# A decode block on one core: two more engines run the attention loop, queries pass through two fixed tiles, and GpSimd's relays go

## The chip, the cores and the metric

The kernel runs on one core of one Trainium2 chip. The metric is device time of one execution in microseconds (us), lower is better. The engines are TensorE (PE in the profile; PEld is its weight load), VectorE (DVE), ScalarE (ACT), GpSimd (POOL) and SyncE (SP, which issues nearly all DMA loads). A trailing q, as in "DVEq", is an engine's sequencer.

## The reference, cut to what matters

```python
# B=2 sequences, one new token each; D=512; 32 query and 32 KV heads of 128; 8192 cached keys
q = layernorm(x) @ wq
scores = einsum("bhqd,bhkd->bhqk", q, k_cache) * 128**-0.5
o = einsum("bhqk,bhkd->bhqd", softmax(scores), v_cache)
h = x + o.reshape(B, 1, 4096) @ wo
y = layernorm(h)                                  # then a gated feed-forward block
g = y @ W_gate
return h + ((g * (g > 0)) * (y @ W_up)) @ W_down    # F = 1376
```

K and V are 134 MB each in bf16 and are read once. The arithmetic per byte is small.

## The kernel before

The 64 (sequence, head) problems are done as 32 "pairs" of two heads. Each pair has a K load and a V load of 4.2 MB each, into four slots (K into slots 0 and 2, V into 1 and 3). Of the 128 key columns per partition, VectorE computes 96 (a mult by the broadcast query, four halving adds, a reduce), and TensorE computes 32 (transposes, which ScalarE copies out of PSUM, then score matmuls). ScalarE takes the exponentials and TensorE multiplies by V ("PV"). Pairs 0 to 29 are a loop of 15 rounds on TensorE alone, while the other engines are unrolled. Pairs 30 and 31 are a separate tail, followed by the output projection and the feed-forward block.

```python
# TensorE, loop (before): GpSimd's semaphores g2p (query copied) and v2p (a K or V load has landed)
with nc.Fori(0, NI, engines=OrderedEngineSet([nc.tensor.engine])):
    k_part(body, 0, (1, 2, 3, 4), ((g2p, 1), (v2p, 1)))
    collect(body, 6)
    pv(body, 0, ((jd, J, ((v2p, 2), (a2p, 5))), (0, jd, ((a2p, 7),))))
    ...
# TensorE, tail: straight on the load's own semaphore
collect(tail, 1)
k_part(tail, P0, (2, 3, 4, 5), ((slot_sem[0], 256), (g2p, 1)))
...                                      # output projection of the first 30 heads
k_part(tail, P1, (9, 10, 11, 12, 14, 15, 16, 17), ((slot_sem[2], 256), (g2p, 2)))

# VectorE, unrolled, pair p
if p == P0:                              # pair 30: first the output of the last loop round
    o_norm(g - 1, t_ob_loop)             # waits for TensorE's collect
    o_spread(g - 1, dve)
dve.wait((slot_sem[s], 16 * (g + 1)), t_q_b)
dve.last()
...                                      # qv: the pair's query, broadcast
t_dm[p] = dve.run(nc.vector.tensor_tensor(out=prod[:, 0:jd, :], in0=k_t[:, 0:jd, :], in1=qv, op=ALU.mult))
...                                      # adds, reduce
# GpSimd, pair p: relays
for k in range(2):
    nc.gpsimd.wait_ge(slot_sem[s + k], 16 * (g + 1))
    nc.gpsimd.sem_inc(v2p, 1)
# SyncE, pair p: the slot is loaded again when the mult and TensorE's transposes have read it
sp.wait(t_dm[p], tokp("pt", p, NG - 1))
load(s, A_k_cache, p + 2)
```

The softmax here doesn't subtract the row's maximum and nothing guards it: scores larger than these inputs give would overflow.

Of the kernel before, what the change touches and what calls it, by code (L numbers as in the profile page):

```python
# [7 lines left out]
F32 = mybir.dt.float32  # L8
# [31 lines left out]
def bass_sequential_preLN__gqa_block_cached__glu_gated_reglu__decode_kernel(  # L40
# [34 lines left out]
    with ExitStack() as es:  # L75
# [15 lines left out]
        a2p, l2p, g2p, v2p = S("a2p"), S("l2p"), S("g2p"), S("v2p")  # L91
# [12 lines left out]
        q_b = sb("q_b", [128, NP * Dh], BF16)  # L104
        qT = sb("qT", [128, NP * 2], BF16)
        q2 = sb("q2", [128, NP, 2, 4], BF16)
        q2c = [sb(f"q2c{i}", [128, 2, 4], BF16) for i in range(2)]
# [12 lines left out]
        NS = 3  # L120
        scores = [sb(f"scores{i}", [128, JC], F32) for i in range(NS)]
# [40 lines left out]
        if True:  # L162

            def program():
# [91 lines left out]
                dve.run(nc.vector.memset(q2[:], 0.0))  # L256
                dve.wait(t)
                dve.last()
                for r in range(2):
                    for h in range(2):  # L260
                        t_q2 = dve.run(nc.vector.tensor_copy(
                            out=q2[64 * h:64 * h + 64, :, r, 2 * h:2 * h + 2],
                            in_=Sp[r][64 * h:64 * h + 64, 0:2 * NP].rearrange("p (n a) -> p n a", a=2)))
# [16 lines left out]
                for m in range(NP // 4):  # L280
                    if m >= 2:
                        dve.wait(t_mm[m - 2])
                    dve.last()
                    t = dve.run(nc.vector.tensor_copy(
                        out=qrep[m % 2].rearrange("p (k r) -> p k r", r=64),
                        in_=qT[:, m * 8:(m + 1) * 8].unsqueeze(2).broadcast_to([128, 8, 64])))
                    if m == 0:
                        t_mm = {}
                    pe.wait(t)
                    if m >= 2:  # L290
                        pe.wait(t_cp[m - 2])
                    for k in range(4):
                        i = nc.tensor.matmul(  # L293
                            Op[m % 2][:, k * 128:(k + 1) * 128], lhsT=qrep[m % 2][:, k * 128:(k + 1) * 128],
                            rhs=ident[:], start=True, stop=True)
                    t_mm[m] = pe.run(i)
                    act.wait(t_mm[m])
                    t_cp[m] = act.run(nc.scalar.activation(  # L298
                        out=q_b[:, m * 512:(m + 1) * 512], in_=Op[m % 2][:], func=ACT.Copy))
# [7 lines left out]
                                        skip_group_check=True))  # L307

# [17 lines left out]
                def k_part(T, p, ev, k_wait):  # L326
                    s, ng = (2 * p) % 4, split(p)[0]
                    k_t = tile(s)
                    wait = nc.tensor.wait_ge

                    def score(g):
                        wait(a2p, ev[g])
                        kv_ = kT[g % 2][:].rearrange("p (k n r) -> p k r n", n=128, r=2)
                        for k in range(GT // 2):
                            jj = g * GT + 2 * k
                            for r in range(2):
                                i = nc.tensor.matmul(  # L337
                                    Sp[p % 2][:, 2 * jj:2 * jj + 4], lhsT=kv_[:, k, r, :],
                                    rhs=q2c[p % 2][:, r, :], start=(r == 0), stop=(r == 1))
                        T.mark(("sc", p, g), i)  # L340
# [3 lines left out]
                    for g in range(ng):  # L344
# [7 lines left out]
                        T.mark(("pt", p, g), i)  # L352
# [4 lines left out]
                def pv(T, p, parts, between=None):  # L357
# [4 lines left out]
                    for j0, j1, waits in parts:  # L362
# [5 lines left out]
                        for j in range(j0, j1, VJ):  # L368
# [4 lines left out]
                                start=(q == 0 and n < 4), stop=(q == PG - 1 and n >= J // VJ - 4))  # L373
                            n += 1
                    T.mark(("pv", p), i)

                def collect(T, a):
# [5 lines left out]
                    T.mark("ob", i)  # L383

                def z_sum(T, bank):
                    T.mark("z", nc.tensor.matmul(  # L386
                        bank[:, ZC:ZC + 8], lhsT=ones_f[:], rhs=zs[:], start=True, stop=True))
# [9 lines left out]
                with nc.Fori(0, NI, engines=OrderedEngineSet([nc.tensor.engine])):  # L397
                    jd = split(0)[1]
                    k_part(body, 0, (1, 2, 3, 4), ((g2p, 1), (v2p, 1)))
                    collect(body, 6)  # L400
                    pv(body, 0, ((jd, J, ((v2p, 2), (a2p, 5))), (0, jd, ((a2p, 7),))))
                    k_part(body, 1, (8, 9, 10, 11), ((g2p, 2), (v2p, 3)))
# [3 lines left out]
                    pv(body, 1, ((jd, J, ((v2p, 4), (a2p, 12))), (0, jd, ((a2p, EV),))))  # L406
                    z_sum(body, Ob)
                    nc.tensor.sem_inc(g2p, -2)
                    nc.tensor.sem_inc(v2p, -4)
# [9 lines left out]
                k_part(tail, P0, (2, 3, 4, 5), ((slot_sem[0], 256), (g2p, 1)))  # L419
# [10 lines left out]
                for c in range(DC):  # L430
# [3 lines left out]
                k_part(tail, P1, (9, 10, 11, 12, 14, 15, 16, 17), ((slot_sem[2], 256), (g2p, 2)))  # L434
                pv(tail, P0, ((j30, J, ((slot_sem[1], 256), (a2p, 6))), (0, j30, ((a2p, 13),))))
                pv(tail, P1, ((j31, J, ((sem_vl[0], 16), (a2p, 18))), (0, j31, ((a2p, 19), (sem_vl[1], 16)))),
                   lambda: z_sum(tail, Sp[0]))
# [7 lines left out]
                def tokp(kind, p, *g):  # L445
                    return tok((kind, p) + g, p // 2)
# [17 lines left out]
                def normalize(bank, t_z):  # L464
                    dve.wait(t_z)
                    dve.run(nc.vector.tensor_reduce(
                        out=zr[:], in_=bank[:, ZC:ZC + 8].rearrange("p (n k) -> p n k", k=2), axis=AX.X, op=ALU.add))
                    dve.last()
                    dve.run(nc.vector.reciprocal(out=zi[:], in_=zr[:]))
                    dve.last()  # L470
# [7 lines left out]
                t_oc = {}  # L478

                def o_norm(g, t_ob):  # L480
                    normalize(Ob, t_ob)
                    t_oc[g] = dve.run(o_scale())

                def o_spread(g, prog):
                    e = prog.eng
                    prog.wait(t_oc[g], tok("og", g))
# [14 lines left out]
                def q_copy(p):  # L501
                    pool.wait(tokp("sc", p - 2, NG - 1) if p >= 2 else t_q2)
                    nc.gpsimd.tensor_copy(out=q2c[p % 2][:], in_=q2[:, p]).then_inc(g2p, 1)  # L503
# [5 lines left out]
                for p in range(NP):  # L509
                    s = (2 * p) % 4  # L510
                    k_t = tile(s)
# [3 lines left out]
                    if p == P0:  # L515
                        o_norm(g - 1, t_ob_loop)
                        o_spread(g - 1, dve)
                    dve.wait((slot_sem[s], 16 * (g + 1)), t_q_b)
                    dve.last()
                    qv = q_b[:, p * Dh:(p + 1) * Dh].unsqueeze(1).broadcast_to([128, jd, Dh])  # L520
                    t_dm[p] = dve.run(nc.vector.tensor_tensor(  # L521
                        out=prod[:, 0:jd, :], in0=k_t[:, 0:jd, :], in1=qv, op=ALU.mult))
                    w = Dh
                    while w > 8:
                        half = w // 2
                        dve.last()
                        dve.run(nc.vector.tensor_tensor(  # L527
                            out=prod[:, 0:jd, 0:half], in0=prod[:, 0:jd, 0:half], in1=prod[:, 0:jd, half:w], op=ALU.add))
                        w = half
                    dve.last()  # L530
                    sc = scores[p % NS]
                    t_s[p] = dve.run(nc.vector.tensor_reduce(out=sc[:, 0:jd], in_=prod[:, 0:jd, 0:w], axis=AX.X, op=ALU.add))  # L532
                    if p % 2 == 0 and 2 <= p < P0:
                        o_norm(g - 1, tok("ob", g))

                    if p < P0:
                        for k in range(2):
                            nc.gpsimd.wait_ge(slot_sem[s + k], 16 * (g + 1))
                            nc.gpsimd.sem_inc(v2p, 1)  # L539
                    if p % 2 == 0 and 2 <= p < P0:  # L540
                        o_spread(g - 1, pool)
                    if p < P1:
                        q_copy(p + 1)

                    def evacs(g0=0, g1=ng):
                        for gg in range(g0, g1):
# [3 lines left out]
                            elif p >= 1:  # L550
                                act.wait(tokp("sc", p - 1, NG - 2 + gg))
                            to_pe(nc.scalar.activation(  # L552
                                out=kT[gg % 2][:], in_=Tp[gg % 2][:].bitcast(BF16), func=ACT.Copy))

                    def exp_pe():
                        act.wait(tokp("sc", p, ng - 1), t_const)
                        exp(p, 0, lambda h, a: Sp[p % 2][h, 0:2 * ng * GT].rearrange(
                            "p (g j a) -> p g j a", a=2, j=VJ)[:, :, :, a])

                    def exp_dve(p, jd):  # L560
                        act.wait(t_s[p])
                        exp(p, 1, lambda h, a: scores[p % NS][h, 0:jd].rearrange("p (g j) -> p g j", j=VJ))

                    def sums():
                        if p >= 1:
                            act.wait(tokp("pv", p - 1))
                        to_pe(nc.scalar.activation(out=os_sb[:], in_=Op[0][:], func=ACT.Copy))  # L567

                    if p < P0:
                        evacs()  # L570
                        exp_pe()
                        if p % 2 == 0:
                            sums()
                        exp_dve(p, jd)
                    elif p == P0:
                        sums()
                        evacs()
                        exp_pe()
# [6 lines left out]
                    else:  # L585
                        evacs(0, NG)
                        exp_dve(P0, j30)
                        evacs(NG)
                        exp_pe()
                        exp_dve(P1, j31)  # L590

                    if p + 2 < NP:
                        sp.wait(t_dm[p], tokp("pt", p, NG - 1))
# [26 lines left out]
                normalize(Sp[0], tok("z", NI))  # L620
                to_pe(nc.scalar.activation(out=os_sb[:], in_=Op[0][:], func=ACT.Copy))
# [142 lines left out]
```

## Time and profile before

| | before |
|---|---|
| time, median of the first 3 runs | 662.32 us |
| DMA engines busy, per round of two pairs (38.85 us) | 1.00, at 431 to 432 GB/s |
| VectorE, TensorE, ScalarE busy per round | 28.7, about 19.5, 11.7 us |
| from a K load's issue to its landing | 32.3 us |

These are lines of the page of the kernel before. "busy us" gives each engine's busy time, its share and its instructions. The two rows of digits give, for 40 equal slices of the run, TensorE's granted clock in tenths and the busy share of the DMA engines. The last line is the chain of waits, by engine. The nines at the start of the clock row are not borne out by the work: from 84.2 to 123.1 us the view of stretches gives a clock of 1.00, but TensorE's 182 matmuls there take 20.38 us, as long as in a round at 0.50 (20.37 us).

```profile
span 660.9 us, 7674 instructions
...
PE 338.3 (51%) x3220; PEld 208.2 (31%) x3220; DVE 465.6 (70%) x282; ACT 198.9 (30%) x418; POOL 22.5 (3%) x121
...
PEclk9999999955556565655655565555565655555567
DMA  9999999999999999999999999999999999999996
...
DMA 80%; DVE 17%; PE 1%; SPq 1%; issue 0%; ACT 0%; DVEq 0%
```

Next is one round in the view of stretches of the kernel before. Its columns are the length, the busy time of each engine with instruction counts, the granted TensorE clock, the DMA share and GB/s.

```profile
core 0: us, PE busy (x) PEld busy (x) DVE busy (x) ACT busy (x) POOL busy (x), PEclk, DMA share, GB/s
...
278.50:317.30 38.80, 20.27 (x182) 12.36 (x174) 28.63 (x16) 11.68 (x25) 1.14 (x7) 0.50 1.00 432
```

The DMA is the only thing in this round with no idle time: a share of 1.00 at 432 GB/s, where VectorE, the busiest of the engines, works 28.63 of 38.80 us.

The timeline of the kernel before, around 290 us, shows how deep the queue is (start, duration, engine, line, operation, and in brackets the idle time before it and what ended that).

```profile
294.21 0.33 SPq L167 DMA_DIRECT2D slot<-in_A_k_cache_dram  x1
...
326.50 6.56 DVE L521 TENSOR_TENSOR prod<-slot,q_b 128x12288 bf16<-128x12288 bf16 x1 [4.63 <-DMA slot<-in_A_k_cache_dram]
...
326.66 1.06 PE L349 MATMUL T<-ident_f,slot 128*128 128x128 f32 x8 [1.69 <-POOLq L539]
```

The K load issued at 294.21 is used at 326.50, though 4.2 MB at 432 GB/s take only 9.7 us. Some 22 us of other loads lie ahead of it, and VectorE has waited 4.63 us for it. The waits of the kernel before, summed (us in total, times, longest), show the same: VectorE waits for K, and GpSimd, the relay, waits for V.

```profile
POOL q2c L503 <- DMA slot<-in_A_v_cache_dram: 221.3, 16, 19.4
...
DVE prod L521 <- DMA slot<-in_A_k_cache_dram: 150.7, 29, 14.2
...
PE T L349 <- POOLq L539: 51.4, 29, 10.3
```

This is the timeline of the tail before: collect (Ob), the transposes of pairs 30 and 31 (T), VectorE's normalization (zr) and mult of pair 30, the PV matmuls (O<-slot,e), and the down-projection (O<-slot,hd).

```profile
617.24 1.87 PE L380 MATMUL Ob<-sel,os_sb 128*128 128x4 f32 x8 [0.18 <-ACT os_sb L567]
...
618.97 1.95 PE L349 MATMUL T<-ident_f,slot 128*128 128x128 f32 x8
619.15 0.17 DVE L466 TENSOR_REDUCE zr<-Ob 128x4 f32<-128x8 f32 x1 [6.19 <-PE Ob L380]
...
620.26 6.55 DVE L521 TENSOR_TENSOR prod<-slot,q_b 128x12288 bf16<-128x12288 bf16 x1
...
632.10 1.69 PE L349 MATMUL T<-ident_f,slot 128*128 128x128 f32 x8
...
643.37 4.06 PE L370 MATMUL O<-slot,e 128*16 128x512 bf16 x48
...
647.68 1.04 PE L370 MATMUL O<-slot,e 128*16 128x512 bf16 x16
...
657.38 1.02 PE L717 MATMUL O<-slot,hd 128*2 128x128 bf16 x24 [0.51 <-DMA slot<-in_B_W_down_dram]
```

At the very end TensorE waits for the last weights: the DMA stream ends the run.

### The profile page before, as it was taken

How to read it: one execution, taken by the hardware profiler on the slowest of the kernel's cores; microseconds unless marked ns; L12 is line 12 of the kernel's file. 1: busy time of each engine (PE TensorE's matmuls, PEld its weight loads, DVE VectorE, ACT ScalarE, POOL GpSimd, SP SyncE). 2: the span in 40 equal slices, each digit the busy share in tenths (PEclk: the TensorE clock that was granted, in tenths of full speed). 3: DMA queues.
4: the chain of work that ended last, by engine and by line, in shares of the span. 5: the costliest groups of instructions: out<-in, count | busy, mean ns of one | idle time of the engine just before them, and what ended most of it. 6: DMA issues, size and time to landing. Idle time of an engine off the chain costs nothing.

```text
span 660.9 us, 7674 instructions
## 1 busy us (share of the span) xinstructions
PE 338.3 (51%) x3220; PEld 208.2 (31%) x3220; DVE 465.6 (70%) x282; ACT 198.9 (30%) x418; POOL 22.5 (3%) x121
## 2 busy tenths in 40 slices
PE   2653354546555354545535464554446454445787
PEld 2431332224333122333313233332324232232464
DVE  1766576788767678776768867676886767787691
ACT  0521321233332133333213333222323322232360
POOL 2000000000000000000000000000000000000000
PEclk9999999955556565655655565555565655555567
DMA  9999999999999999999999999999999999999996
GB/s 381 426 417 428 440 421 438 430 428 438 423 436 432 428 440 420 438 433 424 440 422 436 436 423 438 425 432 436 426 435 428 432 432 430 434 431 428 440 416 270
DMA packets 10787, 281.23 MB, mean 426 GB/s; under 512 B 1202, under 2 KB 1556, under 8 KB 1940
## 3 DMA queue, kind: packets, MB, share of 16 engines
q1 hardware_dynamic: 10760, 281.06, 99.1%
q8 instruction: 6, 0.10, 0.1%
q14 instruction: 9, 0.07, 0.0%
q10 hardware_dynamic: 12, 0.00, 0.0%
HBM read 281.05 MB, written 0.00 MB: 425 GB/s over the span
## 4 chain that ended last, share of the span: by engine, by line
DMA 80%; DVE 17%; PE 1%; SPq 1%; issue 0%; ACT 0%; DVEq 0%
DMA slot<-in_A_k_cache_dram 76%; DVE prod L521 16%; DMA slot<-in_B_W_down_dram 4%; DVE prod L527 1%; PE O L370 0%; PE Ob L380 0%; PE O L717 0%; DVE scores L532 0%; SPq L167 0%; SPq L609 0%; ACT e L457 0%; ACT os_sb L567 0%; SPq L173 0%; SPq L176 0%; SPq L613 0%
## 5 line engine op out<-in xcount | busy, mean ns | idle before, releaser
L521 DVE TENSOR_TENSOR prod<-slot,q_b 128x12288 bf16<-128x12288 bf16 (+1 forms) x32 | 207.7, 6492 | 152.4 <-DMA slot<-in_A_k_cache_dram 150.7
L527 DVE TENSOR_TENSOR prod<-prod 128x6144 bf16<-128x6144 bf16 (+4 forms) x128 | 210.2, 1642 | 4.4
L370 PE MATMUL O<-slot,e 128*16 128x512 bf16 x1024 | 118.2, 615 | 185.5 <-ACT e L457 129.7
L552 ACT ACTIVATE kT<-T 128x1024 bf16<-128x1024 bf16 x132 | 131.2, 1022 | 194.8 <-PE T L349 191.1
L349 PE MATMUL T<-ident_f,slot 128*128 128x128 f32 x528 | 126.7, 401 | 51.4 <-POOLq L539 51.4
L349 PEld LDWEIGHTS T<-ident_f,slot 128*128 128x128 f32 x528 | 91.6, 206 | 65.7 <-issue 65.7
L370 PEld LDWEIGHTS O<-slot,e 128*16 128x16 bf16 x1024 | 26.1, 112 | 251.8 <-ACT e L457 157.3
L457 ACT ACTIVATE e<-scores 64x96 bf16<-64x96 f32 (+1 forms) x64 | 19.4, 303 | 210.2 <-DVE scores L532 209.8
L337 PE MATMUL S<-q2c,kT 128*128 128x4 bf16 x1056 | 50.0, 169 | 37.6 <-ACT kT L552 37.5
L337 PEld LDWEIGHTS S<-q2c,kT 128*128 128x128 bf16 x1056 | 43.3, 107 | 66.5 <-ACT kT L552 64.6
L380 PE MATMUL Ob<-sel,os_sb 128*128 128x4 f32 x136 | 31.0, 351 | 24.9 <-ACT os_sb L567 24.2
L380 PEld LDWEIGHTS Ob<-sel,os_sb 128*128 128x128 f32 x136 | 29.5, 320 | 26.8 <-ACT os_sb L567 25.6
L532 DVE TENSOR_REDUCE scores<-prod 128x96 f32<-128x768 bf16 (+1 forms) x32 | 30.2, 945 | 1.1
L457 ACT ACTIVATE e<-S 64x32 bf16<-64x32 f32 (+1 forms) x64 | 13.0, 204 | 14.8 <-PE S L337 14.4
L503 POOL COPY q2c<-q 128x8 bf16<-128x8 bf16 x32 | 7.6, 238 | 235.3 <-DMA slot<-in_A_v_cache_dram 221.3
L457 ACT ACTIVATION_READ_ACCUMULATOR e<-S 64x1 f32 x64 | 12.8, 201 | 0.7
L489 POOL MEMSET O_l<- 128x40 bf16 (+1 forms) x13 | 1.8, 136 | 315.4 <-DVE O_cur L473 315.4
L457 ACT ACTIVATION_READ_ACCUMULATOR e<-scores 64x1 f32 x64 | 11.8, 184 | 0.0
L386 PEld LDWEIGHTS Ob<-zs,ones_f 128*128 128x128 f32 x30 | 7.2, 300 | 12.7 <-issue 12.7
L567 ACT ACTIVATE os_sb<-O 128x512 f32<-128x512 f32 x16 | 9.6, 597 | 3.2 <-PE O L370 2.8
L298 ACT ACTIVATE q_b<-O 128x512 bf16<-128x512 f32 x8 | 4.3, 594 | 17.9 <-PE O L293 17.9
L386 PE MATMUL Ob<-zs,ones_f 128*128 128x8 f32 x30 | 8.6, 361 | 0.0
(93 smaller groups left out, 83.6 us busy)
## 6 DMA issues: line engine op xcount, KB each, us to landing
slot<-in_A_k_cache_dram SPq DMA_DIRECT2D x32, 4096.0 KB, 32.3
slot<-in_A_v_cache_dram SPq DMA_DIRECT2D x31, 4096.0 KB, 30.6
slot<-in_A_wq_dram SPq DMA_DIRECT2D x1, 4096.0 KB, 12.4
slot<-in_A_v_cache_dram SPq DMA_DIRECT2D x2, 2048.0 KB, 28.0
X<-in_A_wo_dram SPq DMA_DIRECT2D x1, 3840.0 KB, 46.9
slot<-in_B_W_up_dram SPq DMA_DIRECT2D x1, 1376.0 KB, 23.7
slot<-in_B_W_gate_dram SPq DMA_DIRECT2D x1, 1376.0 KB, 26.7
slot<-in_B_W_down_dram SPq DMA_DIRECT2D x2, 512.0 KB, 28.8
```

Source lines behind the costliest of these rows:

```text
L337: i = nc.tensor.matmul(Sp[p % 2][:, 2 * jj:2 * jj + 4], lhsT=kv_[:, k, r, :], rhs=q2c[p % 2][:, r, :], start=(r == 0), stop=(r == 1))
L349: i = nc.tensor.transpose(Tp[g % 2][:, k * 128:(k + 1) * 128], k_t[:, j:j + 2, :].rearrange("p j d -> p (j d)").bitcast(F32), ident_f[:])
L370: i = nc.tensor.matmul(Op[0][c:c + 16, :], lhsT=e_t[q][:, j // VJ, :], rhs=v_t[:, j:j + VJ, :].rearrange("p j d -> p (j d)"), start=(q == ...
L380: i = nc.tensor.matmul(Ob[:, 0:4], lhsT=os_sb[:, jj * Dh:(jj + 1) * Dh], rhs=sel[:, 4 * jj:4 * jj + 4], start=(jj == 0), stop=(jj == VJ - 1))
L386: T.mark("z", nc.tensor.matmul(bank[:, ZC:ZC + 8], lhsT=ones_f[:], rhs=zs[:], start=True, stop=True))
L457: i = nc.scalar.activation(out=e_t[q][h, j0 // VJ:j1 // VJ, 8 * q:8 * q + 8].rearrange("p g (j a) -> p g j a", a=2)[:, :, :, a], in_=src(h ...
L503: nc.gpsimd.tensor_copy(out=q2c[p % 2][:], in_=q2[:, p]).then_inc(g2p, 1)
L521: t_dm[p] = dve.run(nc.vector.tensor_tensor(out=prod[:, 0:jd, :], in0=k_t[:, 0:jd, :], in1=qv, op=ALU.mult))
L527: dve.run(nc.vector.tensor_tensor(out=prod[:, 0:jd, 0:half], in0=prod[:, 0:jd, 0:half], in1=prod[:, 0:jd, half:w], op=ALU.add))
L532: t_s[p] = dve.run(nc.vector.tensor_reduce(out=sc[:, 0:jd], in_=prod[:, 0:jd, 0:w], axis=AX.X, op=ALU.add))
L552: to_pe(nc.scalar.activation(out=kT[gg % 2][:], in_=Tp[gg % 2][:].bitcast(BF16), func=ACT.Copy))
L567: to_pe(nc.scalar.activation(out=os_sb[:], in_=Op[0][:], func=ACT.Copy))
```

## The change

The intent is to put VectorE and ScalarE into the same 15-round loop, so that the program is short. The loop body is written with fixed addresses, the same in every round. The query of a pair (8 columns for TensorE, 128 for VectorE) is therefore copied by GpSimd into one of two fixed tiles, and waits count inside a round and are reset at its end. VectorE itself now tells TensorE that K has landed (k2p), and TensorE waits for V directly. GpSimd relays nothing any more. The core of the diff:

```diff
-        q_b = sb("q_b", [128, NP * Dh], BF16)
+        QW = 8 + Dh
+        q_all = sb("q_all", [128, NP, QW], BF16)
-        q2c = [sb(f"q2c{i}", [128, 2, 4], BF16) for i in range(2)]
+        q_c = [sb(f"q_c{i}", [128, QW], BF16) for i in range(2)]
 ...
-                    k_part(body, 0, (1, 2, 3, 4), ((g2p, 1), (v2p, 1)))
+                    k_part(body, 0, (1, 2, 3, 4), ((k2p, 1),))
 ...
-                k_part(tail, P0, (2, 3, 4, 5), ((slot_sem[0], 256), (g2p, 1)))
+                k_part(tail, P0, (2, 3, 4, 5), ((k2p, 1),))
-                k_part(tail, P1, (9, 10, 11, 12, 14, 15, 16, 17), ((slot_sem[2], 256), (g2p, 2)))
+                k_part(tail, P1, (9, 10, 11, 12, 14, 15, 16, 17), ((k2p, 2),))
 ...
+                with nc.Fori(0, NI, engines=OrderedEngineSet([nc.vector.engine])):
+                    for q in range(PG):
+                        nc.vector.wait_ge(g2d, q + 1)
+                        nc.vector.wait_ge(slot_sem[2 * q], 16)
+                        nc.vector.sem_inc(k2p, 1)
+                        last_d()
+                        run_d(k_mult(q))
+                        last_d()
+                        nc.vector.sem_inc(d2s, 1)
+                        k_adds(q, run_d, last_d)
+                        if q == 0:
+                            nc.vector.wait_ge(p2d, 1)
+                            normalize(Ob, run_d, last_d)
 ...
+                        run_d(k_reduce(q))
+                        last_d()
+                        nc.vector.sem_inc(d2a, 1)
+                    for sem, n in ((d2d, n_d[0]), (g2d, PG), (p2d, 1), (slot_sem[0], 16), (slot_sem[2], 16)):
+                        nc.vector.sem_inc(sem, -n)
 ... (ScalarE: the same kind of loop over evacuations and exponentials)
-                    if p < P0:
-                        for k in range(2):
-                            nc.gpsimd.wait_ge(slot_sem[s + k], 16 * (g + 1))
-                            nc.gpsimd.sem_inc(v2p, 1)
 ... (VectorE, tail, pairs 30 and 31)
+                    if p >= P0:
+                        if p == P0:
+                            dve.wait(t_ob_loop)
+                            normalize(Ob, dve.run, dve.last)
+                            o_spread(g - 1, dve, dve.run(o_scale()))
+                        nc.vector.wait_ge(g2d, p - P0 + 1)
+                        nc.vector.wait_ge(slot_sem[s], 16)
+                        nc.vector.sem_inc(k2p, 1)
 ...
-                        sp.wait(t_dm[p], tokp("pt", p, NG - 1))
+                        sp.wait((d2s, p + 1), tokp("kf", p))
```

## The prediction

> **What bounds the kernel now.** The DMA engines. The table of busy time by stretches of 19.4 us (one pair) shows a DMA share of 1.00 and 429 to 432 GB/s in all thirty stretches from 45 to 628 us. [...] The page's 281.23 MB at 432 GB/s are 651 us (an estimate) of the span of 660.9; the rest is the start (381 GB/s) and about 3 us after the last weights land.
>
> All compute idles in each period. VectorE is busy 14.2 us of 19.4 per pair (mult 6.56, adds 3.36, 1.76, 0.96, 0.56, reduce 0.95); in the waits it waits 150.7 us for K over 29 mults. TensorE is busy 9.8, ScalarE 5.8. The queue is deep: in the timeline a K load is issued right after the mult that frees its slot (294.21) and lands 32.3 us later, though moving its 4 MB takes 9.7. Some 22 us of other loads lie ahead of it: a slot freed up to 20 us later would not starve the DMA.
>
> **What the change does.**
> - VectorE and ScalarE run 15 rounds of a loop. Bytes and tensor work stay; the loop adds a branch, five semaphore resets on VectorE and two on ScalarE per round of 38.85 us. Estimate from the gaps of dependent instructions (0.02 to 0.05 us each): below 1 us a round, inside VectorE's 4.6 to 5.1 us idle per pair.
> - Normalization (0.15 + 0.18 + 0.16 us, about 0.55 with gaps) moves ahead of the reduce of even pairs; exp and the second part of PV come 0.6 us later there. PV now ends at 325.0, the next K lands at 326.5: still in time.
> - TensorE's transposes are released by VectorE reaching the pair, not by GpSimd. VectorE already waits when K lands.
> - The K slot is released at group 2's first score rather than after the last transposes: about 1 us later.
> - GpSimd copies 136 instead of 8 elements per pair (0.19 to 0.34 us now, perhaps 0.4), a pair ahead. Its waits for V (221 us) cost nothing.
> - The mult reads its query 16 bytes into a fixed tile. [...] I expect 6.56 us; no trace here shows it yet. [...]
>
> **On the critical path:** practically nothing. The chain names K loads 76% and the mult 16%, but that mult time passes while the queue is full.
>
> **Prediction:** 662.3 us, 8 in 10 between 661.2 and 664.0. Faster by over 2%: 0.01; within 2%: 0.97; slower by over 2%: 0.02.
>
> **What would show it.** Right: DMA share 1.00 at 432 GB/s in every pair, 38.85 us per round, mult 6.56 us, VectorE waiting for K 4 to 5 us per pair, TensorE's "POOLq" waits gone, last weights landing near 657. Wrong: a stretch with DMA share below 1, mult near 13 us, VectorE idle before a mult for GpSimd's copy or instruction fetch.
>
> **What would make it wrong.** Refetching a loop body behind a saturated DMA, costing over 5 us per pair; GpSimd's query copy, VectorE and TensorE taking turns instead of running a pair ahead; a later tail on VectorE, whose last exp (645.2) precedes V's last half (647.4) by only 2 us.

Two passages are cut from it, and the cuts marked, because no trace or run here shows what they state: a figure for the highest DMA rate, and an argument about the query's offset in its tile with what the mult would cost if it failed. Neither was a term of the forecast. The 662.3 us are the 662.32 us of the kernel before with nothing added, since all extra work was put into idle time. As to the risk of refetching: the pages do list instruction fetches among the DMA queues (15 packets, 0.17 MB before; 10 packets, 0.13 MB after), but that a loop body is fetched again in each round is shown by no trace.

## The result, and the profile after

| | before | after |
|---|---|---|
| time, median | 662.17 us (4 runs, 661.84 to 662.89) | 663.80 us (4 runs, 663.57 to 664.15) |
| ratio | | 1.0024, 95% interval 1.0006 to 1.0041 |

A ratio here is the mean time of one kernel's runs over that of the other's of the same rounds, so it is not quite the ratio of the medians. In the later sets the recorded ratios come out only if the profiled run of the edited kernel is left out (for e1_p0_early, below, its slowest: with it the means give 1.0017 instead of 1.0011). 663.80 lies inside the predicted 661.2 to 664.0, in its upper part. The 1.6 us are still worth a search.

The page of the changed kernel, the same lines as before:

```profile
span 662.3 us, 7890 instructions
...
PE 331.6 (50%) x3221; PEld 200.0 (30%) x3221; DVE 467.6 (71%) x285; ACT 215.9 (33%) x432; POOL 71.9 (11%) x121
...
PEclk9995565555756556755555567555675555557557
DMA  9999999999999999999999999999999999999995
...
DMA 76%; DVE 16%; PE 5%; ACT 2%; issue 1%; SPq 0%; DVEq 0%; ACTq 0%
```

One round of the changed kernel, in the view of stretches:

```profile
278.50:317.30 38.80, 20.35 (x178) 12.33 (x174) 28.73 (x16) 12.95 (x26) 4.53 (x7) 0.50 1.00 432
```

The round is the same: DMA share 1.00, 432 GB/s, VectorE 28.7 us. Two things are new and idle-filling. ScalarE is busy 1.3 us longer and GpSimd 3.4 us longer. Both are in the timeline of the changed kernel:

```profile
294.13 0.33 SPq L168 DMA_DIRECT2D slot<-in_A_k_cache_dram  x1
294.19 6.74 DVE L529 TENSOR_TENSOR prod<-prod 128x6144 bf16<-128x6144 bf16 x4
294.23 3.48 POOL L516 COPY q_c<-q_all 128x136 bf16<-128x136 bf16 x1 [10.90 <-DVEq L572]
...
302.78 1.28 ACT L547 ACT_TABLE_LOAD   x1
...
321.89 0.30 POOL L516 COPY q_c<-q_all 128x136 bf16<-128x136 bf16 x1
...
326.31 1.97 PE L358 MATMUL T<-ident_f,slot 128*128 128x128 f32 x8 [0.61 <-DVEq L568]
326.34 6.56 DVE L520 TENSOR_TENSOR prod<-slot,q_c 128x12288 bf16<-128x12288 bf16 x1 [4.28 <-DMA slot<-in_A_k_cache_dram]
```

The mult takes 6.56 us as before. VectorE still waits 4.28 us for K, and TensorE's transposes start at the same moment as the mult. The same query copy on GpSimd takes 0.30 us once and 3.48 us the other time, when it starts 0.04 us after VectorE's first add (3.36 us) and ends 0.16 us after it; in the whole run 15 copies take 3.48 us. The four adds are not slower for it (6.74 us, and 6.73 us before). ScalarE now loads its function table in every round (15 loads of 1.28 us in the loop, where the kernel before had one). Neither cost shows in the DMA column.

The waits of the changed kernel answer to those of before. GpSimd's waits for V are gone, VectorE's for K are nearly as long, and TensorE's transposes wait for VectorE's sequencer, in the loop and once in the tail (L620).

```profile
DVE prod L520 <- DMA slot<-in_A_k_cache_dram: 142.9, 29, 14.1
...
PE T L358 <- DVEq L568: 29.1, 28, 9.9
...
PE T L358 <- DVEq L620: 0.9, 1, 0.9
```

The last loop round is not late: the mult of pair 29 starts at 598.36 us (before: 598.62). So the extra time is in the tail. The timeline of the tail after:

```profile
617.13 1.87 PE L394 MATMUL Ob<-sel,os_sb 128*128 128x4 f32 x8 [0.17 <-ACT os_sb L550]
...
619.03 0.17 DVE L482 TENSOR_REDUCE zr<-Ob 128x4 f32<-128x8 f32 x1 [6.25 <-PE Ob L394]
...
619.95 1.97 PE L358 MATMUL T<-ident_f,slot 128*128 128x128 f32 x8 [0.95 <-DVEq L620]
...
620.14 6.55 DVE L520 TENSOR_TENSOR prod<-slot,q_c 128x12288 bf16<-128x12288 bf16 x1
...
633.62 1.97 PE L358 MATMUL T<-ident_f,slot 128*128 128x128 f32 x8
...
645.16 4.88 PE L382 MATMUL O<-slot,e 128*16 128x512 bf16 x48
...
650.29 1.04 PE L382 MATMUL O<-slot,e 128*16 128x512 bf16 x16
...
658.58 1.28 PE L791 MATMUL O<-slot,hd 128*2 128x128 bf16 x40
```

TensorE waits 0.95 us for VectorE to finish normalizing and spreading, and the down-projection no longer waits for a landing. The two tails, step by step (starts of the same instructions):

| step | before | after | difference |
|---|---|---|---|
| transposes of pair 30 start | 618.97 | 619.95 | +0.98 |
| from there to the transposes of pair 31 | 13.13 | 13.67 | +0.54 |
| from there to PV of pair 30 | 11.27 | 11.54 | +0.27 |
| from there to the last 16 PV matmuls | 4.31 | 5.13 | +0.82 |
| from there to the first down-projection matmul (656.17, 658.52) | 8.49 | 8.23 | -0.26 |
| from there to the end (device times of these two runs, 662.11 and 663.57) | 5.94 | 5.05 | -0.89 |

The sum is +1.46 us, the difference of the two profiled runs. The first line is the wait. The next four (+1.37) go mostly with TensorE's granted clock; about 0.13 us of the +0.54 is pair 31 held by VectorE (13.67 us, against 13.54 in f3_both below, without that gate at the same half speed). Between 628 and 633 us it was 0.84 before and 0.50 after; between 643 and 650 us, 0.78 and 0.54; between 650 and 657 us, 0.71 and 0.95. The last line is the wait for weights (0.51 us on TensorE's matmuls and 0.33 on its weight load), which is gone because TensorE now comes later. So, as an estimate from these lines, TensorE's chain could have been about 0.9 us later before the change at no cost.

### The profile page after: what moved, and what is told of

It reads as the page before. It is cut to its first block, busy times and chain, and to the rows that moved or that the text cites. A ratio compares the mean times of both kernels' runs of the same rounds, so it can differ in the third digit from the quotient of the medians. Undisturbed runs are those within 1.5% of the kernel's fastest.

```text
span 662.3 us, 7890 instructions
## 1 busy us (share of the span) xinstructions
PE 331.6 (50%) x3221; PEld 200.0 (30%) x3221; DVE 467.6 (71%) x285; ACT 215.9 (33%) x432; POOL 71.9 (11%) x121
## 4 chain that ended last, share of the span: by engine, by line
DMA 76%; DVE 16%; PE 5%; ACT 2%; issue 1%; SPq 0%; DVEq 0%; ACTq 0%
DMA slot<-in_A_k_cache_dram 76%; DVE prod L520 15%; PE O L382 1%; PE T L358 1%; DVE prod L529 1%; ACT kT L547 1%; PE O L442 1%; PE Ob L394 0%; PE S L341 0%; PE W L448 0%; ACT e L474 0%; PE O L739 0%; PE S L739 0%; PE O L791 0%; ACT os_sb L550 0%
## 5 line engine op out<-in xcount | busy, mean ns | idle before, releaser
L520 DVE TENSOR_TENSOR prod<-slot,q_c 128x12288 bf16<-128x12288 bf16 (+1 forms) x32 | 207.7, 6492 | 144.9 <-DMA slot<-in_A_k_cache_dram 142.9
L358 PE MATMUL T<-ident_f,slot 128*128 128x128 f32 x528 | 117.6, 379 | 30.2 <-DVEq L568 29.1
L358 PEld LDWEIGHTS T<-ident_f,slot 128*128 128x128 f32 x528 | 84.7, 194 | 45.6 <-DVEq L568 44.5
L516 POOL COPY q_c<-q_all 128x136 bf16<-128x136 bf16 x32 | 57.1, 1788 | 198.2 <-DVEq L572 168.0
L341 PE MATMUL S<-q_c,kT 128*128 128x4 bf16 x1056 | 49.2, 169 | 39.2 <-ACT kT L547 38.5
L341 PEld LDWEIGHTS S<-q_c,kT 128*128 128x128 bf16 x1056 | 41.1, 105 | 68.0 <-ACT kT L547 66.6
L299 ACT ACTIVATE q_all<-O 128x512 bf16<-128x512 f32 x8 | 4.4, 596 | 17.9 <-PE O L294 17.9
## 6 DMA issues: line engine op xcount, KB each, us to landing
slot<-in_A_k_cache_dram SPq DMA_DIRECT2D x32, 4096.0 KB, 32.1
```

Of the source, the lines that this page charges most:

```text
L341: i = nc.tensor.matmul(Sp[p % 2][:, 2 * jj:2 * jj + 4], lhsT=kv_[:, k, r, :], rhs=q_c[p % 2][:, 4 * r:4 * r + 4], start=(r == 0), stop=(r ...
L358: i = nc.tensor.transpose(Tp[g % 2][:, k * 128:(k + 1) * 128], k_t[:, j:j + 2, :].rearrange("p j d -> p (j d)").bitcast(F32), ident_f[:])
L516: nc.gpsimd.tensor_copy(out=q_c[p % 2][:], in_=q_all[:, p]).then_inc(g2d, 1)
L520: return nc.vector.tensor_tensor(out=prod[:, 0:jd_, :], in0=tile((2 * p) % 4)[:, 0:jd_, :], in1=q_c[p % 2][:, 8:QW].unsqueeze(1).broadcast ...
```

## The experiments

**Theory A:** TensorE's tail has two new gates. Pair 30 waits for VectorE's normalization and spread of the last round. Pair 31 waits until VectorE has got through pair 30 (its reduce starts at 633.50, TensorE's pair 31 at 633.62). They make TensorE's chain, and not the DMA, end last. **Theory L:** the loops cost it, a little per round (table loads, longer copies, branches). **Theory C:** it is only where TensorE's full-speed stretches fall in the tail.

### First set, one chip: the gates removed, and the gates alone

e1_p0_early, the edit in the changed kernel:

```diff
+                        nc.vector.wait_ge(g2d, p - P0 + 1)
+                        nc.vector.wait_ge(slot_sem[s], 16)
+                        nc.vector.sem_inc(k2p, 1)
                         if p == P0:
                             dve.wait(t_ob_loop)
                             normalize(Ob, dve.run, dve.last)
                             o_spread(g - 1, dve, dve.run(o_scale()))
-                        nc.vector.wait_ge(g2d, p - P0 + 1)
-                        nc.vector.wait_ge(slot_sem[s], 16)
-                        nc.vector.sem_inc(k2p, 1)
```

> The changed kernel, but in the tail VectorE releases TensorE for pair 30 before it normalizes and spreads the last loop round's output, not after. Theory A (the 1.5 us come from the tail: TensorE's chain there ends last, because both its pairs are now released by VectorE's program order): pair 30's transposes start near 619.0 us instead of 619.95, but pair 31's still wait until VectorE has dispatched pair 30's reduce (633.5), so the time stays within 0.4 us of the changed kernel (663.8). Theory L (the loops cost it, a little in each round): same time as the changed kernel, and the same for the next two kernels. Theory C (nothing but the phase of TensorE's granted clock in the tail): no change that is owed to the edit; the time follows the clock that the profile shows after 618 us.

e2_both_early does the same for pair 30, and in VectorE's adds of pair 30:

```diff
+                        if p == P0 and w == Dh // 4:      # second add issued
+                            nc.vector.wait_ge(g2d, 2)
+                            nc.vector.wait_ge(slot_sem[2], 16)
+                            nc.vector.sem_inc(k2p, 1)
```

> As e1_p0_early, and pair 31 is released after pair 30's second add was issued (about 630 us). Theory A: pair 31's transposes start near 632.6 instead of 633.6, the chain of TensorE ends about 1 us earlier: 662.2 to 663.0, near the kernel before (662.2). Theory L: 663.8 as the changed kernel. Theory C: 663.8, moved only by the clock.

e3_before_gated puts the two gates, and nothing else, into the kernel before:

```diff
-                k_part(tail, P0, (2, 3, 4, 5), ((slot_sem[0], 256), (g2p, 1)))
+                k_part(tail, P0, (2, 3, 4, 5), ((slot_sem[0], 256), (g2p, 1), (k2p, 1)))
 ... (pair 31 likewise, with (k2p, 2))
                     dve.wait((slot_sem[s], 16 * (g + 1)), t_q_b)
+                    if p >= P0:
+                        nc.vector.sem_inc(k2p, 1)
```

> The kernel before, no loops on VectorE and ScalarE, no fixed query tile, GpSimd's relays kept; TensorE only waits in the tail, in addition, until VectorE has reached pair 30 (after normalization and spread) and pair 31. Theory A: 0.7 to 1.6 us slower than the kernel before, near 663.5, and TensorE no longer waits for the down-projection weights. Theory L and theory C: same time as the kernel before (662.2) within 0.3 us, apart from the clock.

| run | this, median (range) | kernel before, same rounds | ratio, 95% interval |
|---|---|---|---|
| e1_p0_early | 663.11 (662.10 to 664.53) | 662.03 | 1.0011 (0.9998 to 1.0025) |
| e2_both_early | 661.29 (660.79 to 661.62) | 662.03 | 0.9985 (0.9971 to 0.9998) |
| e3_before_gated | 663.26 (661.91 to 663.48) | 662.03 | 1.0011 (0.9998 to 1.0025) |

Removing both gates took more than the whole 1.6 us away with the loops, table loads and copies still in place; at 661.29 it is even below the 662.2 to 663.0 that theory A had allowed. Adding the gates to the kernel before, which has none of those, made it about 1 us slower, though the interval just reaches 1. That speaks for A and against L. In the trace of e3_before_gated the wait appears where A puts it (timeline), and the wait for the down-projection weights is gone, as expected:

```profile
619.70 1.94 PE L350 MATMUL T<-ident_f,slot 128*128 128x128 f32 x8 [1.01 <-DVEq L521]
```

In e1_p0_early the transposes of pair 30 started at 619.02, as expected, and those of pair 31 were held by VectorE until 633.79 (timeline). What pair 30 gained, pair 31 gave back.

```profile
619.02 1.95 PE L358 MATMUL T<-ident_f,slot 128*128 128x128 f32 x8
...
633.79 1.97 PE L358 MATMUL T<-ident_f,slot 128*128 128x128 f32 x8 [1.09 <-DVEq L616]
```

The median, 0.7 us under the changed kernel's first result, missed the expected 0.4. But e1's times run over 2.4 us, so an effect of half a microsecond can't be read from five of them.

### Is the slack of the loop real? Extra work on VectorE

e4_pad3, in the loop of the changed kernel, puts half a mult in front of the mult; e5_pad7 instead issues run_d(k_mult(q)) and last_d() once more. The edit of e4_pad3:

```diff
+                        run_d(nc.vector.tensor_tensor(
+                            out=prod[:, :, 0:64], in0=tile(2 * q)[:, 0:JC, 0:64],
+                            in1=q_c[q][:, 8:72].unsqueeze(1).broadcast_to([128, JC, 64]), op=ALU.mult))
+                        last_d()
                         run_d(k_mult(q))
                         last_d()
```

> The changed kernel with an extra half mult on VectorE in each of the 30 loop pairs (about 3.36 us, result overwritten by the full mult). By the account that VectorE has 4.3 to 5 us idle per pair and K's slot some 20 us of queue slack: rounds stay 38.85 us apart with DMA share 1.00, and only the last round's 3.4 us show in the tail: 666 to 668 us. If time followed VectorE's work per round instead (no slack): 663.8 + 30 x 3.4 = 765 us.

> The changed kernel with the full mult issued twice in each of the 30 loop pairs: VectorE needs about 21.0 us per pair, over the 19.4 that the DMA needs. By the account: VectorE becomes the limit, never waits for K after the first rounds, DMA share falls to about 0.92, and the time to 700 to 715 us (26 + 30 x 21 + 50).

e4_pad3 took 667.00 us (665.67 to 667.49), a ratio of 1.0068 (1.0052 to 1.0083). That is 3.2 us over the changed kernel for 101 us of added VectorE work. The same stretch as above, in e4_pad3:

```profile
278.50:317.30 38.80, 17.26 (x178) 9.75 (x174) 35.44 (x18) 12.74 (x26) 4.54 (x7) 0.63 1.00 432
```

VectorE is busy 35.44 of 38.80 us and the DMA share is still 1.00. Only the last round's extra half mult, which nothing follows in the loop, reaches the end: TensorE's collect in the tail starts at 620.19, 3.06 us later than in the changed kernel. This bears out the prediction's account of the loop for VectorE, and it speaks against theory L: the extra work of 29 pairs vanishes. It does not test ScalarE's slack, where the table loads are. For those the evidence is the DMA share of 1.00 in every round, pair 29 starting no later than before, and e2_both_early, which keeps them all and is not slower than the kernel before.

e5_pad7 went over the slack, as meant, and missed its number: 743.49 us (one run, state unknown), not 700 to 715. VectorE became the limit and the DMA share fell to 91.9%. The VectorE timeline of e5_pad7, two starts of a round's first mult and the second pair's between them:

```profile
294.86 13.15 DVE L520 TENSOR_TENSOR prod<-slot,q_c 128x12288 bf16<-128x12288 bf16 x2 [1.24 <-DVEq L586]
...
316.89 13.15 DVE L520 TENSOR_TENSOR prod<-slot,q_c 128x12288 bf16<-128x12288 bf16 x2 [0.29 <-POOL q_c L516]
...
339.14 13.15 DVE L520 TENSOR_TENSOR prod<-slot,q_c 128x12288 bf16<-128x12288 bf16 x2 [1.23 <-DVEq L586]
```

A round takes 44.28 us, 22.14 a pair, where I had put 21.0. The missing 1.1 us a pair are the normalization (0.76 us a round), the idle time at the round's end (1.24 us), 0.29 us between its two pairs, which is a wait for GpSimd's query copy, and gaps. Thirty pairs times 1.1 us are 34 of the 37 us between the time and the sum 26 + 30 x 21 + 50. So the loop's end, with its five semaphore resets, does cost VectorE about 1.2 us per round here, and in the changed kernel that lies in idle time (VectorE waits 5.00 us for K before a round's first mult, at 306.91 us).

### Second and third set: is it the gates or the clock?

r1_after_again is the changed kernel unedited, and r2_e1_again is the kernel of e1_p0_early. Both ran on a second chip together with e6_late_small.

> The changed kernel, nothing edited, beside the next two on one chip, and a second profile of its tail. Theory A: again about 1.6 us over the kernel before, TensorE's transposes of pair 30 after VectorE's spread, the end set by TensorE and not by a landing. If the granted clock in the tail falls differently than in its first profile (half from 616 to 649.7), the time should move by up to 1 us with it.

> The kernel of e1_p0_early again, to tell its 663.1 from the changed kernel's 663.8 on one chip. Theory A: within 0.4 us of r1_after_again, since pair 31 still waits for VectorE's reduce of pair 30. If it is clearly faster (over 0.4 us), releasing pair 30 alone has a worth that the account misses.

e6_late_small is e2_both_early with two small loads moved from the start to behind the last V load. The reason is a line of the timeline of e2_both_early: TensorE, early now, waits 2.03 us for the last half of V.

```profile
641.54 2.77 PE L382 MATMUL O<-slot,e 128*16 128x512 bf16 x48
...
646.65 1.67 PE L382 MATMUL O<-slot,e 128*16 128x512 bf16 x16 [2.03 <-DMA slot<-in_A_v_cache_dram]
```

```diff
-                nc.sync.dma_start(wo_last[:]...).then_inc(sem_wl, 16)      # at the start
-                nc.sync.dma_start(wd_last[:], ...).then_inc(sem_wd[3], 16)
 ... (after both halves of V of pair 31)
+                        nc.sync.dma_start(wo_last[:]...).then_inc(sem_wl, 16)
+                        nc.sync.dma_start(wd_last[:], ...).then_inc(sem_wd[3], 16)
```

> As e2_both_early, and the loads of the last two heads' output weights and the last 96 rows of the down-projection (352 KB) are issued behind V of pair 31 instead of at the start. If the end of e2_both_early is set by the landing of V's last half (TensorE waited 2.0 us for it), that half lands 0.8 us earlier (estimate: 352 KB at 432 GB/s), and the time falls by 0.3 to 0.9 us, to about 660.6, unless the down-projection weights then land last. If TensorE or VectorE sets the end, no change.

A third chip then ran all four combinations of the two gates side by side. f2_p1_only is e2_both_early with pair 30's release back behind the spread.

> The changed kernel again, first corner of a table of four on one chip: pair 30 released late or early, pair 31 released late or early. Theory A: about 663.4, TensorE's output projection of the FFN (the start of the down-projection matmuls) some 5.0 us before the time, as in all profiles of kernels whose end TensorE sets.

> Second corner: only pair 30 released early. Theory A as first put says within 0.4 us of f0_none; the two earlier sets of five gave 0.7 less on average. If it is again 0.4 to 0.9 us less, the account has to be widened (pair 30's gate moves where the full-speed stretches of TensorE's clock fall, or gives time that pair 31's gate does not take back); if not, the earlier difference was the clock's chance.

> Third corner: pair 30 released late as in the changed kernel, only pair 31 early. Theory A: TensorE gets to pair 31 at about 633.6 by itself, so its early release is worth nothing alone: within 0.3 us of f0_none.

> Fourth corner: both early. Theory A: 661.3 again, about 2 us under f0_none, more than the two single edits together, because each gate hides behind the other.

| set | run | this, median (range) | before, median | ratio, 95% interval |
|---|---|---|---|---|
| second | r1_after_again | 663.00 (662.58 to 663.66) | 661.95 | 1.0019 (1.0005 to 1.0032) |
| second | r2_e1_again | 662.24 (662.18 to 663.07) | 661.95 | 1.0005 (0.9992 to 1.0019) |
| second | e6_late_small | 661.08 (660.65 to 661.15) | 661.95 | 0.9982 (0.9969 to 0.9996) |
| third | f0_none | 662.65 (660.51 to 663.60) | 662.14 | 0.9996 (0.9980 to 1.0012) |
| third | f1_p0_only | 663.07 (662.15 to 663.85) | 662.14 | 1.0012 (0.9999 to 1.0024) |
| third | f2_p1_only | 662.44 (661.29 to 663.86) | 662.14 | 1.0004 (0.9992 to 1.0016) |
| third | f3_both | 662.26 (661.27 to 662.97) | 662.14 | 0.9998 (0.9985 to 1.0011) |

The third set did not bear out the clear picture of the first. The same changed kernel ran twice in 660.5 to 660.6 us and four times in 662.6 to 663.6. The kernel with both gates removed was no faster there than with them, where about 2 us had been expected. So I had taken the first set for more than it was. In the second set r2_e1_again was 0.76 us under r1_after_again, outside the expected 0.4; in the third, f1_p0_only was 0.42 us above f0_none. No gain from pair 30 alone is left of that. f2_p1_only lay 0.2 us from f0_none, as expected. Pooled over the three chips (mean, standard error, range):

| kernel | runs | mean | range |
|---|---|---|---|
| before | 33 | 662.18 ± 0.07 | 661.62 to 663.14 |
| changed (first result, r1, f0) | 15 | 662.95 ± 0.28 | 660.51 to 664.15 |
| pair 30 early (e1, r2, f1) | 15 | 662.90 ± 0.20 | 662.10 to 664.53 |
| pair 31 early (f2) | 6 | 662.44 ± 0.38 | 661.29 to 663.86 |
| both early (e2, f3) | 10 | 661.76 ± 0.23 | 660.79 to 662.97 |
| before with the gates (e3) | 5 | 662.98 ± 0.29 | 661.91 to 663.48 |

The pooled order is the one theory A expects: pair 30 alone is worth nothing, both together about 1.2 us, with a standard error near 0.4. It is carried by the first chip, and by comparisons across chips.

The spread comes, at least in part, from TensorE's clock. In the timelines every profile of the changed kernel (first, r1, f0) has the same wait of 0.95 us in front of pair 30, and f0_none has 0.43 us more in front of pair 31. Two lines of f0_none, then pair 31 of f3_both, which does not wait:

```profile
619.23 1.09 PE L358 MATMUL T<-ident_f,slot 128*128 128x128 f32 x8 [0.95 <-DVEq L620]
...
632.89 1.97 PE L358 MATMUL T<-ident_f,slot 128*128 128x128 f32 x8 [0.43 <-DVEq L620]
...
632.18 1.95 PE L358 MATMUL T<-ident_f,slot 128*128 128x128 f32 x8
```

What differs is the clock, which the view of stretches gives for each part of the tail:

| profile | pair 30 starts | clock 628 to 633 | 633 to 643 | 643 to 650 | 48 PV matmuls take | first down-projection matmul | time of that run |
|---|---|---|---|---|---|---|---|
| before | 618.97 | 0.84 | 0.50 | 0.78 | 4.06 | 656.17, then waits for weights | 662.11 |
| changed, first | 619.95 | 0.50 | 0.50 | 0.54 | 4.88 | 658.52 | 663.57 |
| r1_after_again | 619.68 | 0.71 | 0.56 | 0.65 | 4.47 | 657.61 | 662.58 |
| f0_none | 619.23 | 0.50 | 0.50 | 0.64 | 4.50 | 657.63 | 662.69 |
| e1_p0_early | 619.02 | 0.80 | 0.52 | 0.50 | 5.28 | 659.37 | 664.53 |
| f3_both | 618.64 | 0.50 | 0.50 | 0.61 | 5.12 | 657.58 | 662.63 |
| e2_both_early | 617.68 | 0.50 | 0.82 | 0.78 | 2.77 | 656.58 | 661.62 |

e2_both_early and f3_both are one and the same kernel. Its two profiles differ by 1.0 us in time. In one, the clock was full from 636 to 647 us and 48 PV matmuls took 2.77 us; in the other they took 5.12 us. But the 2.77 us are not what made that run faster: TensorE then waited 2.03 us for V. Its lead was there at pair 31, which started 1.44 us earlier (630.74, f3_both 632.18), because its full-speed stretch from 616 to 619 us shortened the collect (1.05 us, f3_both 1.87) and pair 30's transposes. And e1_p0_early, which had lost its wait at pair 30, was the slowest of all: its pair 31 was held until 633.79, the latest of all, and its PV ran wholly at half speed. The last column is the one before it plus 5.0 to 5.2 us in every row but the first, so in those TensorE's chain sets the end.

The traces show the gates more clearly than the times do. From the start of the collect to the start of pair 31's transposes, TensorE needs, by which gates are in and by the speed of the clock during the collect:

| gates in the kernel | collect at half speed | collect at full speed |
|---|---|---|
| none | 15.27 us (f3), 15.26 (e6) | 13.97 (e2) |
| pair 30 only | no profile | 15.10 (f2) |
| pair 31 only | 16.49 (e1), 16.49 (f1) | 15.68 (r2) |
| both | 16.49 (first), 16.49 (r1) | 15.68 (f0) |

So the gates delay TensorE by 1.2 to 1.7 us, the same to 0.01 us on three chips. (The kernel before took 14.86 us, with a full-speed stretch before pair 31, and 16.55 us with both gates put in, in e3_before_gated.) Pair 31's gate alone costs as much as both: VectorE's own way through pair 30 then sets the time, which is why releasing pair 30 alone gained nothing. What follows pair 31, up to the first down-projection matmul, takes 24.07 to 25.84 us, by the clock and the wait for V. That varies as much as the gates cost, and it is why the times of one set need not show them.

In the tails the view of stretches, in steps of 1 us, shows full-speed stretches with lengths of 3.4, 6.8 and once 10.2 us. They fall differently from run to run of the same kernel: from 628 to 633 us the changed kernel had a clock of 0.50 in its first profile and 0.71 in r1_after_again. What starts one is not shown: in the first profile TensorE was busy for 22.3 of the 27 us from 616 to 643 and the clock stayed at 0.50 throughout. That the place of these stretches is why one kernel spreads over 3 us here was not tested. It is an inference from the table.

Part of e6_late_small's expectation came true: its median and mean are the lowest of all (0.9982 of the kernel before), although two single runs of f0_none (660.51 and 660.63 us) were lower still. The expected mechanism was not shown. In its profile the 48 PV matmuls ran at half speed (4.89 us), TensorE did not wait for V at all, and the time was 661.08 us. What its trace shows instead is that the whole stream ran earlier once the small loads were out of its way: pair 29's mult starts at 597.09 us (597.92 to 598.62 in the profiles of before, e1, e3, r1, r2, f0 to f3), and TensorE's collect at 615.86 (616.68 to 617.30). It is the best version measured, on one chip, by 0.2%; I do not claim more for it.

## Why the prediction was right or wrong

- **"The DMA engines bound the kernel; practically nothing of the change is on the critical path": right for the loop.** DMA share 1.00 and 431 to 432 GB/s in every round from 84 us on, and the start of pair 29 within 0.3 us. e4_pad3 shows the slack directly, and e5_pad7 shows where it ends.
- **"TensorE's transposes are released by VectorE reaching the pair. VectorE already waits when K lands": right for the 30 pairs of the loop, wrong for the tail.** There K of pair 30 had landed at about 617.7 us (issued at 585.58, 32.1 us to landing), about 2.3 us before TensorE's transposes started, and VectorE stood waiting for TensorE's collect, with normalization and spread still to do. The release of pair 30 came 0.95 us late (trace, three profiles), and that of pair 31 waited until VectorE was through pair 30: 16.49 us after the collect, without the gates 15.27. This is the step that failed. It was small because, before, TensorE still had about 0.9 us to wait for the last weights: an estimate from these numbers is that 0.3 of the 1.2 us reach the end with that slack, and all of it where a slower clock has used the slack up. The number held because this step was small, not because it was foreseen.
- **"A later tail on VectorE" as a risk: wrong engine.** VectorE's mult of pair 31 was even 0.2 us earlier (634.49, before 634.68). The tail of TensorE was later.
- **"Loop below 1 us a round": somewhat too low.** e5_pad7 shows 1.24 us idle at the end of a round, where the gaps of dependent instructions that the estimate rested on are 0.02 to 0.05 us. It lies in VectorE's idle time.
- **Normalization ahead of the reduce, "0.6 us later": 0.9 us.** The exponentials of an even pair start 15.24 us after its mult (306.91 to 322.15), before 14.34 (307.07 to 321.41). No effect on the DMA.
- **K slot released "about 1 us later": not so.** K is issued 0.1 us after the mult's end (294.13), as before. The mult still ends last.
- **GpSimd's copy "perhaps 0.4 us": 0.30 us alone, 3.48 us in every second pair**, where it runs beside VectorE's first add. Why it takes so long there is not shown. Not on the path.
- **The mult at 6.56 us: right.** This shows only that the mult keeps its time with its query 16 bytes into the tile; it tests no other offset. ScalarE's 15 table loads were not foreseen at all; hidden.
- **The size.** The predicted median of 662.3 was 1.5 us under the first result and 0.65 us under the pooled mean of the changed kernel (662.95). One step is known from the traces: the gates. What else the traces show to vary is where the full-speed stretches of the clock fall. What decides that, and how much of the mean difference of 0.8 us each of the two makes, stays open.

## What to carry to other kernels

When a transfer queue is kept full by 20 us of outstanding loads, as here, an edit of a compute engine in the loop can cost and gain nothing until that engine's own work per round passes the transfer time (VectorE at 35.4 of 38.8 us lost nothing in the loop, with a full extra mult a round took 44.28 us); look at the first and last rounds instead. When a relay is replaced by a signal from a busy engine, check every place where that engine has other work in front of the signal: here the loop had none, and the tail had a normalization and the whole of pair 30. And before believing differences of 0.2%, run the same kernel on more than one chip: five runs with a tight spread gave a clear story that five on a third chip did not repeat. Where the times are too noisy, compare the distance between the same two instructions in several traces.
